# Row factor of the attention probabilities folded into their two float16 passes (units 16 to 47)

## The chip, the cores and the metric

The kernel runs on one core of one Trainium2 chip. The metric is device time in microseconds of one execution of the whole program. [...]

## The reference

Three stages follow each other: a windowed attention, a first feed-forward layer, and a second one with its own normalisation.

```python
# q, k, v: 4 x 8 x 576 x 64; heads 0 to 3: window of 32; heads 4 to 7: the same, dilated by 4
scores = where(mask, scale * q @ k.T, -1e9)
attn = exp(scores - max(scores)); attn = attn / (sum(attn) + 1e-9)
x = (attn @ v) as 2304 x 512
h = x @ w_in                    # 512 x 2048
x = (h - tanh(h)) @ w_out       # 2048 x 512
h = x @ w_in2                   # 512 x 1024
sm = softmax(h); solu = h * sm
out = (layer_norm(solu) * g_ln) @ w_out2
```

## The kernel before

The 2304 tokens are cut into six groups of 384. The attention of a group is eight units, so there are 48 units, and a unit is four blocks of 96 queries by 128 keys. Units 0 to 7 run at the start, alone. All later units run between the matmuls of the first feed-forward layer, by a plan of slots: the layer has 96 steps of two slots, the even slot with the 12 matmuls of `mm1` (L485), the odd one with the 12 of `mm2` (L512, five steps behind). A unit has four slots, and every sixteenth slot holds the products with v of four units (`pv_pe`, L407). Each engine works its instructions off in the order in which the slots issue them.

From unit 16 on, a unit u goes through these stations.

- `prep_unit` (L289 on ScalarE, L290 and L292 on VectorE) makes a high and a low float32r part of q and k (units 20 to 47), tile `qks`.
- `qk_half` (L328, twice per unit, `half0` and `half1`) multiplies them into PSUM, and VectorE adds the mask and takes the row's bound (L337, L340) into the tile `p`.
- `sm_exp` (L348, ScalarE) makes the four blocks of `p` into exponentials, with a row sum each.
- `sm_norm` (L353 and L355 on VectorE) makes the factor `rs` from the sums, one number for each row and block. Then L357 on GpSimd multiplies `p` by it in place, 96x512 in one instruction. For units 16 and up the factor has 2^-14 in it, which `pv_pe` takes out later.
- `p_hi` (L366, ScalarE) casts `p` to float16 into the first half of the tile `pab`, one instruction of 96x512. `p_lo` (L371, VectorE) subtracts that from `p` into the second half, again one of 96x512.
- A transposing DMA (L374, issued by SyncE's queue) brings `pab` into `ptt`, and `p_sum` (L379, VectorE) adds the two parts into `pt`, which TensorE uses in L407.

The plan places `p_hi` one slot and `p_lo` two slots behind `sm_norm`, and `p_sum` three slots behind `p_lo`. `p` and `pab` share a ring of three buffers. As the built program has it, `pab` of a unit takes the buffer that `pab` of the unit before had: `p_hi` of unit u+1 waits for the landing of unit u's transposing DMA.

Beside this, every step of the layer has four passes over 128x384: tanh (L493, ScalarE), a subtraction (L496, VectorE), a cast (L499, ScalarE) and a second subtraction (L502, VectorE), which feed `mm2` five steps later. PSUM has two banks for `mm1`, two that the units' scores and products with v share (released by L340 and by L417), and four for `mm2`.

Units 20 to 39 also carry a load and a maximum over a piece of a later weight (L188, L208). After the sixteen steps of each group the results of `mm2` are copied out (L518, L520) and their maxima taken (L245).

Of the kernel before, what the change touches and what calls it, by code (L numbers as in the profile page):

```python
# [13 lines left out]
AF = mybir.ActivationFunctionType  # L14
ALU = mybir.AluOpType
# [9 lines left out]
NQ, NK = 96, 128  # L25
# [15 lines left out]
def tile_kernel(ctx: ExitStack, tc: tile.TileContext, qk, vw, cst, w_in, w_out, w_in2, w_out2, g_ln, out):  # L41
    nc = tc.nc
# [124 lines left out]
    DT = 2 * NU  # L167
# [183 lines left out]
    def sm_norm(u):  # L351
        d = un[u]
        nc.vector.tensor_scalar(out=d["rs"], in0=d["sm"], scalar1=1e-9, scalar2=2.0 ** -14 if u >= DT else 1.0,  # L353
                                op0=ALU.add, op1=ALU.mult)
        nc.vector.reciprocal(out=d["rs"], in_=d["rs"])  # L355
        eng = nc.vector if u == NU - 1 else nc.gpsimd
        eng.tensor_tensor(out=d["p"], in0=d["p"],  # L357
                          in1=d["rs"].unsqueeze(2).to_broadcast([NQ, 4, NK]), op=ALU.mult)
# [4 lines left out]

    def p_hi(u):
        d = un[u]
        nc.scalar.copy(out=d["ab"][:, 0:4 * NK], in_=d["p"].rearrange("p b k -> p (b k)"))  # L366

    def p_lo(u):
        d = un[u]
        ab = d["ab"]  # L370
        nc.vector.tensor_tensor(out=ab[:, 4 * NK:], in0=d["p"].rearrange("p b k -> p (b k)"), in1=ab[:, 0:4 * NK],  # L371
                                op=ALU.subtract)
        d["tt"] = at_p.tile([NK, 2, 4, NQ], F16, tag="ptt", name=f"ptt{u}")
        nc.sync.dma_start_transpose(out=d["tt"].rearrange("p a b q -> p (a b) q"), in_=ab)  # L374

# [62 lines left out]
    for r in range(NU + 3):  # L438
        t = qk_f32(r, st_ps, "qk") if r < NU else None
        b1 = pv_pe(r - 4, st_ps, "pv") if r % 2 == 0 and 0 <= r - 4 < NU else None  # L440
        b2 = tr_pe(r - 2, st_ps, "tr") if 0 <= r - 2 < NU else None
        if t:
            t()
        if back:
            back("h")
        if t:
            sm_exp(r)
        if 0 <= r - 1 < NU:
            sm_norm(r - 1)
        if back:  # L450
            back("l")
        back = b1
        if b2:
            b2()
        if r in SW:
            w_step(dve=True)
        if r in (4, 5):
            load_v(r + 2)
        if r in (6, 8):
            load_unit(NU + r // 2 - 3)  # L460
# [76 lines left out]
    def plan():  # L537
# [3 lines left out]
        for u in range(u0, u1 + 2):  # L541
            p = 4 * u - 41 if u >= 2 * NU else (2, 6, 8, 12, 14, 16, 18, 20)[u - u0]
            q = p + 2 if u >= 2 * NU or u < u0 + 4 else p + 1
            if u < u1:
                at(p + 1, lambda u=u: preps.extend(prep_unit(u + 1)))
                for i in (1, 1, 2):
                    at(p + i, lambda: preps.pop(0)() if preps else None)
                if u < NFU:
                    piece(p, lambda u=u: qk_f32(u, a_ps, "at"))
                    at(p + 1, lambda u=u: sm_exp(u))  # L550
                    at(p + 2, lambda u=u: sm_norm(u))
                else:
                    piece(p, lambda u=u: qk_half(u, 0, a_ps, "at"))
                    at(p + 2, lambda u=u: sm_exp(u, (0, 1)))
                    piece(p + 1, lambda u=u: qk_half(u, 1, a_ps, "at"))
                    at(p + 3, lambda u=u: sm_exp(u, (2, 3)))
                    at(p + 4, lambda u=u: sm_norm(u))
                i = u - NFU
                if 0 <= i < 20:
                    at(p - 1, lambda u=u, i=i: sc_load(u + 2, i))  # L560
                    at(p + 1, lambda u=u, i=i: sc_max(u + 2, i))
                if i == 20:
                    at(p - 1, lambda u=u: new_qk(u + 2))
                    at(p - 1, lambda u=u: sc_rows(u + 2))
                    piece(p + 1, lambda: sc_pe(a_ps, "at"))
                at(p + 1, lambda u=u: load_unit(u + 2))
            if DT <= u < u1:
                for i, fn in ((3, p_new), (5, p_hi), (6, p_lo), (9, p_sum)):
                    at(p + i, lambda u=u, fn=fn: fn(u))
# [497 lines left out]
```

## Time and profile before

| | us |
|---|---|
| median of 3 runs (lowest, highest) | 682.93 (682.88, 683.92) |
| the profiled execution | 683.13 |
| its span | 681.3 |
| TensorE busy | 661.0 (97%) |
| VectorE busy | 532.6 (78%) |
| ScalarE busy | 386.3 (57%) |
| GpSimd busy | 174.5 (26%) |

The changed instructions lie between 110 and 410 us of the span. The busy time of an engine is the union of its instructions' times; consecutive instructions of one engine overlap a little, so distances from start to start are shorter than durations.

### The profile page before, as it was taken

To read this page: it belongs to the slowest core of one execution; us is meant where nothing else is said; L and a number is where in the kernel's file an instruction comes from. 1 tells how busy PE (TensorE), PEld (TensorE's weight loads), DVE (VectorE), ACT (ScalarE), POOL (GpSimd) and SP (SyncE) were. 2 spreads that over 40 slices of the span, in tenths; PEclk is the share of its full clock that TensorE was granted. 3 is DMA by queue.
4 is the path that set the end of the run, shared out by engine and by line. 5 is a ranking of instruction groups with operands and counts; after the bars stand their busy time and mean duration, and the time that the engine had idled before them with its cause. 6 is when DMAs were issued, how large, how long until landed. Compare 5 with 4: busy or idle time off the path is not lost. (4 is left out here: it accounts for less than half of the span.)

```text
span 681.3 us, 11184 instructions
## 1 busy us (share of the span) xinstructions
PE 661.0 (97%) x3882; PEld 547.9 (80%) x3882; DVE 532.6 (78%) x1315; ACT 386.3 (57%) x917; POOL 174.5 (26%) x174
## 2 busy tenths in 40 slices
PE   6998999999999999999999999999999999999997
PEld 5787899999999999999999999999954444444443
DVE  5988657679888997999888963499978877777751
ACT  5778757545555655555565532475636645555442
POOL 2302311110111110101111010266314656644411
PEclk9999989999999999999999999999999999999999
DMA  9977632254545555454434211453412555433233
GB/s 284 353 233 213 199 105 55 82 158 117 141 121 149 159 147 149 126 176 107 110 93 110 54 25 49 146 192 124 155 46 63 124 124 123 94 81 74 67 89 92
DMA packets 93608, 87.09 MB, mean 128 GB/s; under 512 B 62192, under 2 KB 78064, under 8 KB 93552
## 3 DMA queue, kind: packets, MB, share of 16 engines
q1 hardware_dynamic: 90384, 81.67, 43.5%
q10 hardware_dynamic: 3168, 4.72, 1.9%
q8 instruction: 30, 0.49, 0.3%
q14 instruction: 26, 0.21, 0.1%
HBM read 62.25 MB, written 9.44 MB: 105 GB/s over the span
## 5 line engine op out<-in xcount | busy, mean ns | idle before, releaser
L485 PE MATMUL h<-x,wi 128*128 128x384 f32 x1152 | 218.7, 339 | 0.8 <-DVE t L496 0.8
L512 PE MATMUL y<-gs,wo 128*128 128x384 f32 x1152 | 217.9, 339 | 0.0
L485 PEld LDWEIGHTS h<-x,wi 128*128 128x128 f32 x1152 | 201.1, 190 | 2.1 <-DVE t L496 1.0
L512 PEld LDWEIGHTS y<-gs,wo 128*128 128x128 f32 x1152 | 200.0, 189 | 1.9 <-issue 0.3
L357 POOL TENSOR_TENSOR p<-p,rs 96x512 f32<-96x512 f32 x47 | 58.6, 1247 | 341.8 <-DVE rs L355 328.8
L502 DVE TENSOR_TENSOR gs<-t,gs 128x384 fp32r<-128x384 f32 x96 | 81.1, 845 | 22.7 <-ACT gs L499 22.7
L931 PE MATMUL po<-w2o_o,zt 128*128 128x512 f16 x432 | 94.8, 379 | 0.0
L499 ACT CAST gs<-t 128x384 fp32r<-128x384 f32 x96 | 48.9, 510 | 76.5 <-DVE t L496 76.3
L348 ACT ACTIVATE p<-p,nm 96x128 f32<-96x128 f32 x192 | 74.8, 391 | 19.7 <-DVE nm L313 19.7
L931 PEld LDWEIGHTS <-zt 128*128 128x128 f16 x432 | 42.0, 98 | 51.0 <-DMA zt<-e 0.4
L496 DVE TENSOR_TENSOR t<-h,t 128x384 f32<-128x384 f32 x96 | 53.0, 552 | 33.5 <-ACT t L493 32.8
L779 PEld LDWEIGHTS <-yt 128*128 128x128 f16 x378 | 36.9, 98 | 47.0 <-issue 3.5
L493 ACT ACTIVATE t<-h 128x384 f32<-128x384 f32 x96 | 46.3, 483 | 36.5 <-PE h L485 33.1
L854 ACT ACTIVATE e<-hn,sml 128x1024 f32<-128x1024 f32 x18 | 20.7, 1150 | 56.3 <-DVE sml L794 43.5
L779 PE MATMUL sp<-w2i_t,yt 128*128 128x512 f16 x216 | 48.6, 379 | 2.2 <-DVE u L817 2.2
L904 DVE SCALAR_TENSOR_TENSOR e<-hn,sml,e 128x1024 f16<-128x1024 f32 x18 | 25.6, 1426 | 19.6 <-ACT e L903 19.6
L779 PE MATMUL sp<-w2i_b,yt 128*128 128x512 f16 x162 | 37.9, 379 | 0.0
L308 PE MATMUL qkp<-qkr 64*96 64x128 f32 x160 | 29.9, 343 | 8.0 <-DMA qkr<-in_qk_dram 6.0
L366 ACT CAST pab<-p 96x512 f16<-96x512 f32 x32 | 19.8, 619 | 31.4 <-POOL p L357 23.4
L348 ACT ACTIVATION_READ_ACCUMULATOR p<-p,nm 96x1 f32 x192 | 36.0, 187 | 0.0
L308 PEld LDWEIGHTS qkp<-qkr 64*96 64x96 f32 x160 | 24.5, 208 | 12.6 <-DMA qkr<-in_qk_dram 5.6
L313 DVE CUSTOM_DVE_ANT_0 p<-qkp,cst_sb 96x128 f32<-96x128 f32 x80 | 18.3, 281 | 14.9 <-PE qkp L308 8.2
(116 smaller groups left out, 844.3 us busy)
## 6 DMA issues: line engine op xcount, KB each, us to landing
qkr<-in_qk_dram SPq DMA_DIRECT2D x28, 448.0 KB, 3.4
raw_wi<-in_w_in_dram SPq DMA_DIRECT2D x16, 511.8 KB, 7.0
raw_wo<-in_w_out_dram SPq DMA_DIRECT2D x16, 511.8 KB, 7.6
v<-in_vw_dram SPq DMA_DIRECT2D x48, 128.0 KB, 3.6
y_dr<-ys ACTq DMA_DIRECT2D x6, 768.0 KB, 3.9
yr<-y_dr SPq DMA_DIRECT2D x9, 512.0 KB, 4.2
out_dram<-o SPq DMA_DIRECT2D x18, 256.0 KB, 2.7
qkr<-in_qk_dram SPq DMA_DIRECT2D x20, 224.0 KB, 5.2
```

The lines of the kernel that those rows point to most:

```text
L308: nc.tensor.matmul(ps[:, b], d["r"][:64, b * NQ:(b + 1) * NQ], d["r"][:64, QC + b * NK:QC + (b + 1) * NK], start=True, stop=True)
L348: nc.scalar.activation(out=d["p"][:, b], in_=d["p"][:, b], func=AF.Exp, scale=-1.0, bias=d["nm"][:, b:b + 1], accum_out=d["sm"][:, b:b + 1])
L357: eng.tensor_tensor(out=d["p"], in0=d["p"], in1=d["rs"].unsqueeze(2).to_broadcast([NQ, 4, NK]), op=ALU.mult)
L485: nc.tensor.matmul(ps, w[:, a, k * 128:(k + 1) * 128], xt[g, k][:, b], start=(n == 0), stop=(n == 3 * KD - 1))
L493: nc.scalar.activation(out=t, in_=ps, func=AF.Tanh)
L496: nc.vector.tensor_tensor(out=t, in0=ps, in1=t, op=ALU.subtract)
L499: nc.scalar.copy(out=gs[:, 0], in_=t)
L502: nc.vector.tensor_tensor(out=gs[:, 1], in0=t, in1=gs[:, 0].bitcast(F32), op=ALU.subtract)
L512: nc.tensor.matmul(yb[g][m], wo[c][:, a, m * 128:(m + 1) * 128], gs[:, b], start=(c == 0 and i == 0), stop=(c == NF - 1 and i == 2))
L779: nc.tensor.matmul(ps, y[:, a, blk, kk], w2i[w, kk][:, b], start=first and q == 0, stop=q == 5, skip_group_check=not first)
L904: nc.vector.scalar_tensor_tensor(out=ab[:, 1], in0=d["hn"], scalar=d["f"], in1=ab[:, 0], op0=ALU.mult, op1=ALU.subtract)
L931: nc.tensor.matmul(po, z[:, a, j], w2o[j][:, b], start=(q == 0), stop=(q == 3 * NF2 - 1))
```

## The change

For units 16 and up `sm_norm` stops after the reciprocal, so that GpSimd no longer multiplies `p`, and `p` keeps the plain exponentials. `p_hi` becomes four ScalarE instructions of 96x128, each with the factor of its block as the scale of the activation. `p_lo` becomes four VectorE instructions of 96x128 that multiply by the same factor and subtract the high part in one pass. Units 8 to 15 keep the multiplication on GpSimd. No other instruction is moved.

```diff
--- before.py
+++ after.py
@@ -353,6 +353,8 @@
         nc.vector.tensor_scalar(out=d["rs"], in0=d["sm"], scalar1=1e-9, scalar2=2.0 ** -14 if u >= DT else 1.0,
                                 op0=ALU.add, op1=ALU.mult)
         nc.vector.reciprocal(out=d["rs"], in_=d["rs"])
+        if u >= DT:
+            return
         eng = nc.vector if u == NU - 1 else nc.gpsimd
         eng.tensor_tensor(out=d["p"], in0=d["p"],
                           in1=d["rs"].unsqueeze(2).to_broadcast([NQ, 4, NK]), op=ALU.mult)
@@ -363,13 +365,17 @@
 
     def p_hi(u):
         d = un[u]
-        nc.scalar.copy(out=d["ab"][:, 0:4 * NK], in_=d["p"].rearrange("p b k -> p (b k)"))
+        for b in range(4):
+            nc.scalar.activation(out=d["ab"][:, b * NK:(b + 1) * NK], in_=d["p"][:, b], func=AF.Copy,
+                                 scale=d["rs"][:, b:b + 1])
 
     def p_lo(u):
         d = un[u]
         ab = d["ab"]
-        nc.vector.tensor_tensor(out=ab[:, 4 * NK:], in0=d["p"].rearrange("p b k -> p (b k)"), in1=ab[:, 0:4 * NK],
-                                op=ALU.subtract)
+        for b in range(4):
+            nc.vector.scalar_tensor_tensor(out=ab[:, (4 + b) * NK:(5 + b) * NK], in0=d["p"][:, b],
+                                           scalar=d["rs"][:, b:b + 1], in1=ab[:, b * NK:(b + 1) * NK], op0=ALU.mult,
+                                           op1=ALU.subtract)
         d["tt"] = at_p.tile([NK, 2, 4, NQ], F16, tag="ptt", name=f"ptt{u}")
         nc.sync.dma_start_transpose(out=d["tt"].rearrange("p a b q -> p (a b) q"), in_=ab)
 
```

The order on ScalarE around the high part of unit 30 was this. A name is followed by its unit and a running number; in brackets stand the counters that an instruction waits on. `DMAHW6` counts the landing of unit 29's transposing DMA here: the instruction that adds the transposed parts of unit 29 waits on it too.

```order
L366 CAST pab30_2866<-p30_2773 96x512 [waits DMAHW6_49,Pool_49]
L289 CAST qks32_2919<-qkr32_2758 128x896 [waits DMAHW4_49]
L493 ACTIVATE t42_2906<-h42_2893 128x384 [waits PE_49]
L348 ACTIVATE p31_2881,sm31_2883<-p31_2881,nm31_2882 96x128 [waits DVE_49] x2
L499 CAST gs42_2907<-t42_2906 128x384 [waits DVE_49]
L348 ACTIVATE p31_2881,sm31_2883<-p31_2881,nm31_2882 96x128 x2
```

With the change the same place reads as follows (lines from L374 on have moved by six).

```order
L369 ACTIVATE pab30_2936<-p30_2838,rs30_2841 96x128 [waits DMAHW6_49,DVE_49,Activation_49]
L369 ACTIVATE pab30_2936<-p30_2838,rs30_2841 96x128 [waits Activation_49] x3
L289 CAST qks32_2991<-qkr32_2823 128x896 [waits DMAHW4_49]
L499 ACTIVATE t42_2975<-h42_2962 128x384 [waits PE_49]
L348 ACTIVATE p31_2951,sm31_2953<-p31_2951,nm31_2952 96x128 [waits DVE_49] x2
L505 CAST gs42_2976<-t42_2975 128x384 [waits DVE_49]
```

One instruction has become four, the wait for GpSimd is gone, the wait for the DMA has stayed, and the cast of q and k for unit 32 (L289) still stands right behind. The other waits on ScalarE's own counter are for the exponentials of the same blocks, issued several instructions before.

On VectorE the place of unit 30's low part was this.

```order
L496 TENSOR_TENSOR t42_2906<-h42_2893,t42_2906 128x384 [waits Activation_49]
L371 TENSOR_TENSOR pab30_2866<-p30_2773,pab30_2866 96x512 [waits Pool_49]
L292 TENSOR_TENSOR qks32_2919<-qkr32_2758,qks32_2919 128x512
L502 TENSOR_TENSOR gs42_2907<-t42_2906,gs42_2907 128x384 [waits Activation_49]
L496 TENSOR_TENSOR t43_2962<-h43_2949,t43_2962 128x384 [waits Activation_49]
```

With the change it is this.

```order
L502 TENSOR_TENSOR t42_2975<-h42_2962,t42_2975 128x384 [waits Activation_49]
L376 SCALAR_TENSOR_TENSOR pab30_2936<-p30_2838,rs30_2841,pab30_2936 96x128 x4
L292 TENSOR_TENSOR qks32_2991<-qkr32_2823,qks32_2991 128x512
L508 TENSOR_TENSOR gs42_2976<-t42_2975,gs42_2976 128x384 [waits Activation_49]
L502 TENSOR_TENSOR t43_3037<-h43_3024,t43_3037 128x384 [waits Activation_49]
```

The four passes stand in the place of the one, ahead of L292, which completes the operands of unit 32's scores.

## Rows read from the trace of the kernel before

**Rows 1.** Busy time by stretch: stretch, length, then each engine's busy time, clock, DMA

```profile
110.00:410.00 300.00, 299.99 (x1947) 294.47 (x1946) 253.06 (x703) 167.33 (x467) 35.33 (x33) 1.00 0.44 117
```

**Rows 2.** One line's instructions, GpSimd, L357: duration in ns, least/median/most

```profile
L357 POOL TENSOR_TENSOR p<-p,rs x47: 1037/1039/2378, 10.7 to 401.2; 96x512 f32<-96x512 f32 x47
```

**Rows 3.** Timeline, 240 to 252 us: start, length, engine, line, operation, tiles, [idle before]

```profile
240.86 0.68 DVE L371 TENSOR_TENSOR pab<-p,pab 96x512 f16<-96x512 f32 x1
...
241.46 0.68 DVE L292 TENSOR_TENSOR qks<-qkr,qks 128x512 fp32r<-128x512 f32 x1
241.60 1.21 SPq L374 DMA_TRANSPOSE ptt<-pab  x1
...
242.13 0.55 DVE L502 TENSOR_TENSOR gs<-t,gs 128x384 fp32r<-128x384 f32 x1
...
243.68 1.04 POOL L357 TENSOR_TENSOR p<-p,rs 96x512 f32<-96x512 f32 x1 [7.54 <-DVE rs L355]
...
243.81 1.32 DVE L502 TENSOR_TENSOR gs<-t,gs 128x384 fp32r<-128x384 f32 x1 [0.30 <-ACT gs L499]
244.75 0.62 ACT L366 CAST pab<-p 96x512 f16<-96x512 f32 x1 [0.97 <-POOL p L357]
...
245.28 0.94 ACT L289 CAST qks<-qkr 128x896 fp32r<-128x896 f32 x1
...
246.51 0.56 DVE L290 TENSOR_TENSOR qks<-qkr,qks 64x384 fp32r<-64x384 f32 x1
...
248.98 0.68 DVE L371 TENSOR_TENSOR pab<-p,pab 96x512 f16<-96x512 f32 x1
```

**Rows 4.** Timeline, TensorE, first halves of the scores of units 31 to 34

```profile
243.47 0.40 PE L328 MATMUL qkp<-qks 128*96 128x256 f32 x2
...
252.29 0.40 PE L328 MATMUL qkp<-qks 128*96 128x256 f32 x2
...
261.10 0.40 PE L328 MATMUL qkp<-qks 128*96 128x256 f32 x2
...
271.59 0.40 PE L328 MATMUL qkp<-qks 128*96 128x256 f32 x2
```

**Rows 5.** One line, L374: the transposing DMAs from issue to landing

```profile
DMA to landing us min/median/max: 2.8/2.9/4.8
```

**Rows 6.** Timeline, 148 to 173 us: two high parts that waited for a landing

```profile
148.73 1.21 SPq L374 DMA_TRANSPOSE ptt<-pab  x1
...
153.28 0.62 ACT L366 CAST pab<-p 96x512 f16<-96x512 f32 x1 [2.07 <-DMA ptt<-pab]
...
168.33 1.22 SPq L374 DMA_TRANSPOSE ptt<-pab  x1
...
172.99 0.62 ACT L366 CAST pab<-p 96x512 f16<-96x512 f32 x1 [2.49 <-DMA ptt<-pab]
```

**Rows 7.** Single lines: durations in ns, least/median/most, of like instructions elsewhere

```profile
L627 DVE SCALAR_TENSOR_TENSOR w2o_o<-f,gl,w2o_o x8: 739/744/1229, 460.3 to 494.2; 128x512 f16<-128x512 f32 x8
...
L904 DVE SCALAR_TENSOR_TENSOR e<-hn,sml,e x18: 1271/1285/1744, 513.3 to 665.6; 128x1024 f16<-128x1024 f32 x18
...
L348 ACT ACTIVATE p<-p,nm x192: 384/388/405, 6.8 to 397.8; 96x128 f32<-96x128 f32 x192
```

**Rows 8.** Timeline, 148 to 179 us: VectorE's last work before TensorE's scores

```profile
148.59 0.68 DVE L292 TENSOR_TENSOR qks<-qkr,qks 128x512 fp32r<-128x512 f32 x1
...
149.81 0.40 PE L328 MATMUL qkp<-qks 128*96 128x256 f32 x2
...
159.89 1.02 DVE L417 SCALAR_TENSOR_TENSOR x<-pv,x 128x384 fp32r<-128x384 f32 x2
160.50 0.48 PE L328 MATMUL qkp<-qks 128*96 128x256 f32 x2
...
177.56 0.68 DVE L292 TENSOR_TENSOR qks<-qkr,qks 128x512 fp32r<-128x512 f32 x1
...
178.38 0.45 PE L328 MATMUL qkp<-qks 128*96 128x256 f32 x2
```

## The prediction

> **What bounds the kernel now.** I read the busy time by stretch first. Between 110 and 410 us, where all the changed instructions lie, TensorE works for 299.99 of 300.00 us at its full clock, while VectorE has 253.06, ScalarE 167.33 and GpSimd 35.33 [rows 1]. So in this stage the time is TensorE's instruction stream, and nothing that another engine saves can make it shorter. Another engine can only make it longer, by handing something over too late. The question of this change is therefore: which hand-over to TensorE is tightest, and how do the new passes move it?
>
> TensorE's own rhythm comes from the starts of the units' first scores: 243.47, 252.29, 261.10, 271.59 [rows 4]. A plain unit takes 8.82 us of TensorE, and one with the products with v 10.49. One unit in four is of the second kind, so the mean is (3 x 8.82 + 10.49) / 4 = 9.24 us.
>
> Next I followed one unit through the timeline [rows 3], from the low part of unit 29 (L371, start 240.86) to that of unit 30 (248.98). The point to see there is a loop that goes round once per unit, through three engines. The low part ends at 241.54, and the transposing DMA is issued at 241.60. Its landing frees the buffer into which the next unit's high part (L366) is written, 2.8 to 4.8 us later, median 2.9 [rows 5]. The high part starts at 244.75, L289 behind it at 245.28 (0.53 from start to start), and it runs for 0.94. VectorE needs its result in L290 (246.51), and 2.47 us after L290's start the next low part starts. In sum 0.68 + 0.06 + 2.9 + 0.04 + 0.53 + 0.94 + 0.03 + 2.47 = 7.65 us, with 0.04 and 0.03 as estimates for the hand-overs to ScalarE and VectorE, of the size of the 0.06 between 241.54 and 241.60. That is 1.2 us below TensorE's 8.82, so the loop bounds nothing today, and in the row itself L366 was released by GpSimd, not by the DMA. But twice early in the stage it waited for the landing, 2.07 and 2.49 us [rows 6].
>
> The last thing to see is how little room the hand-over itself has. Behind each low part L292 completes the operands of the scores of two units later. It ends at 149.27 and TensorE's scores start at 149.81; it ends at 178.24 and they start at 178.38 [rows 8]. In the second case the scores start 0.14 after L292's end, which I take as the least distance. In the first there is thus 0.4 us to spare.
>
> **The change part by part.**
>
> *GpSimd's multiplication goes, 32 of the 47 [rows 2].* Its least duration is 1.04 us, but GpSimd is not what TensorE waits for: on that engine it is worth nothing. Two things end with it. L366 no longer waits for it (0.97 us), and L502 no longer runs beside it: L502 took 1.32 us beside GpSimd's instruction, 0.55 without it [rows 3]. That gives VectorE 0.77 us per unit. The cover that makes this worth nothing is TensorE's full stretch [rows 1].
>
> *The low part becomes four passes.* The like instruction, with a factor from memory, float32 in and float16 out, takes 744 ns at 512 elements and 1285 at 1024 [rows 7], that is 1.057 ns per element, so 744 - 384 x 1.057 = 338 ns at 128. On VectorE an instruction starts 0.08 us before its forerunner ends (240.86 + 0.68 against 241.46 [rows 3]). Four passes take 4 x 0.338 - 3 x 0.08 = 1.11 us to the last result against 0.68: **+0.44** in the loop, the same ahead of L292, and the same on VectorE. VectorE as a whole gets shorter (-0.77 + 0.44). Bounds for the four: 0.68 us (no cost per pass, as the one of 512 elements) and 1.35 us (4 x 0.338, no overlap). I take 1.11, since the overlap is seen in the very place.
>
> *The high part becomes four activations.* L348 is the nearest row: 96x128 with an operand per row, 388 ns [rows 7]. ScalarE overlaps by 0.09 us (244.75 + 0.62 against 245.28). L289 then starts 4 x (0.388 - 0.09) = 1.19 us after the first of them instead of 0.53: **+0.66** in the loop. Bounds: 0.53 us (no cost per piece) and 1.55 us (no overlap); I take 1.19 for the same reason. ScalarE itself has the time: 167 of 300 us busy.
>
> *The sum.* The loop becomes 7.65 + 0.44 + 0.66 = **8.75 us** at the median landing, 8.65 at the least, and 10.65 at the longest. TensorE's plain unit is 8.82. What was a margin of 1.2 us is none: every landing above 3.0 us makes the loop late, and it catches up only in the unit with the products. Around it, the end of each group adds copies and maxima (L518, L245) to VectorE's part of the loop, about 2 us in eight units. Units 40 to 47 have no L208 and a loop of some 8.2.
>
> What this costs TensorE I worked through by hand, unit by unit, with the landings of this trace. Unit 19's DMA was issued at 148.73 and its successor's high part waited until 153.28 [rows 6]; now the issue is 0.44 later, the activations take 0.66 more, and unit 20's low part and all behind it on VectorE come 1.1 to 1.5 later. Its L417, which frees a PSUM bank for the scores at 160.50, started at 159.89 [rows 8], and these scores already stand right behind the end of its first instruction. They move by 1.5 us. Unit 21's long landing (168.33 to 172.99 [rows 6]) delays unit 22 by a further 1.1: L292 ends not at 178.24 but near 180.7, TensorE is by then late by 1.5 itself, and loses about 1.0 more. After that the lateness stays and makes room; the next losses are small (0.1 at unit 25, 0.7 and 0.1 at the group ends of units 29 and 37), and a third long landing, at unit 38, costs 1.1. Together 4.5 us. If all landings took 2.9, the first two losses and the last would vanish, and about 1 us would be left at the tight places. Which landings are long is chance (the longest is 1.9 above the median, and I see no cause), so I take 3.0 us, between the two. Behind 410 us TensorE has no idle time that could give it back.
>
> The profiled execution took 683.13 us, 0.2 above the median of the runs. 683.13 + 3.0 = 686.1, against the median 685.9.
>
> [...] The rows at hand give a 128-element pass 338 ns (VectorE) and 388 ns (ScalarE). [...]
>
> **The rivals.**
> *Not slower: the loop stays below TensorE's unit.* VectorE is relieved by 0.77 us per unit and reaches each wait earlier; if the pieces cost half of what I added (0.22 and 0.33) and the landings are mostly at 2.8, the loop is 7.55 + 0.55 = 8.10 us, and TensorE's scores are never late; with the full pieces and no long landing near a tight place only the small losses are left. It decides at 8.82. For it: the row of 241.60 landed in time, and the median landing is 2.9. Against it: rows 6. The time would be 682.9 to 684.3. Even then it is hardly faster: the stretch can give back only what TensorE waits in it, the 0.01 us of rows 1 and the two late starts of rows 8, some 0.3 us together: 682.6.
> *Much slower: the pieces do not overlap.* With 1.35 and 1.55 us the loop is 9.35 at the median landing, above even the mean unit of 9.24. Then TensorE follows the loop. With the group ends' 2 us in eight units, units 20 to 39 would lose 20 x (9.35 + 0.25 - 9.24) = 7.2 us, and the early losses (2.5) come on top: 683.13 + 9.7 = 692.8. Against it: both overlaps are seen wherever two instructions stand side by side.
>
> **How the numbers follow.** A measurement of this kernel can tell about 0.2% (1.4 us) from no change. The forecast, a loop as long as TensorE's unit with losses of 1.4 to 6.5 us, gets 0.60; much slower 0.10; not slower 0.30, of which 0.04 for a time below by more than 0.2% and 0.26 within. That makes 0.04 faster, 0.26 same, 0.70 slower. The range takes in most of the first rival and the forecast's upper end: 683.0 to 690.0.
>
> **What would show it.** Right: four passes with starts 0.26 us apart and four activations 0.30 apart; L502 at 0.55 us everywhere in units 16 to 47; the high part's release changed from GpSimd to the landing in most of units 20 to 39; VectorE's L290 waiting for L289; idle time of TensorE before L328, in the stretch 140 to 340 us most of all; the distance of unit starts above 8.82 in some plain units. Wrong: TensorE at 300 of 300 us as before, or starts of the low parts 8.82 apart or less with landings of 3 us; a loss that lies behind 410 us; or TensorE waiting for another tile than the scores' operands or the bank that L417 frees.

## The result, and the profile after

| us | before | after |
|---|---|---|
| median (lowest to highest, runs) | 683.42 (682.88 to 685.08, 4) | 690.73 (689.43 to 693.07, 4) |
| the profiled execution | 683.13 | 689.43 |
| its span | 681.3 | 687.3 |

The change makes the kernel slower: the ratio is 1.0096, with a 95% interval of 1.0072 to 1.0119. The forecast was 685.9, slower with a chance of 0.70. The side is right; the size was too small, and 690.73 lies 0.7 us above the end of the range.

**Where the 6.0 us of span arose.** I compared the start of TensorE's first matmul of each of the layer's 96 steps in the two traces. The kernel after is 1.62 us late by step 7 (67.77 us in before), and stays at 1.62 until step 21. From step 22 on, in the stage between 140 and 420 us, it falls back a further 4.00. The tail adds 0.4. The first 1.62 lies ahead of the stage: the first changed instruction of the program, the high part of unit 16, already starts 1.5 us late itself.

The first high part in the timeline of the kernel before:

```profile
110.76 0.61 ACT L366 CAST pab<-p 96x512 f16<-96x512 f32 x1
```

In that of the kernel after:

```profile
112.30 1.28 ACT L369 ACTIVATE pab<-p,rs 96x128 f16<-96x128 f32 x4
```

No changed instruction has run by then. What differs is TensorE's granted clock. The row of the kernel before (columns as in [rows 1]), then that of the kernel after:

```profile
61.00:64.40 3.40, 3.40 (x21) 3.26 (x19) 3.15 (x7) 3.16 (x7) 1.91 (x1) 1.00 0.51 199
```

```profile
61.00:64.40 3.40, 3.40 (x13) 3.40 (x12) 3.09 (x7) 3.15 (x7) 1.91 (x1) 0.50 0.24 98
```

In the kernel after the granted clock is 0.50 of full here, and TensorE, busy throughout in both, has 13 matmuls in this stretch where the kernel before has 21. Just before, from 55 to 60 us, it was busy 2.76 and 2.78 of 5 us, the same in both. The kernel before has one such stretch ahead of the stage (86.0 to 89.4 us, 0.50), the kernel after a second one like it (88.3 to 91.7, 0.50) besides this one. It does not hang on the change alone: the profile of the changed kernel with four more loads (below) has full clock from 61 to 64 us, and the kernel before with an unused tile has the half clock there.

In the profiles of the experiments the early lateness lies between -1.1 and 5.2 us (at step 20), and the time of the kernel before scatters as well: 22 later runs of it lay between 682.99 and 688.93. Much of that scatter goes with the clock: of all 63 later runs of it, the 19 with a mean granted clock of 0.997 have a median of 683.39 us, the 33 with 0.994 or 0.995 one of 684.83. So 4.0 us is what this profile charges to the change in the stage, and the repetitions below give 3.6 and 4.4.

**The stage by stretch**, in the changed kernel (columns as in [rows 1]):

```profile
140.00:180.00 40.00, 38.79 (x249) 37.69 (x249) 31.12 (x100) 22.22 (x67) 0.00 (x0) 1.00 0.46 130
180.00:220.00 40.00, 39.30 (x255) 38.54 (x254) 34.16 (x110) 25.33 (x77) 0.00 (x0) 1.00 0.53 146
220.00:260.00 40.00, 40.00 (x260) 39.41 (x259) 33.80 (x112) 25.94 (x79) 0.00 (x0) 1.00 0.51 147
...
300.00:340.00 40.00, 39.51 (x255) 38.48 (x254) 34.50 (x119) 24.40 (x79) 0.00 (x0) 1.00 0.48 128
...
380.00:420.00 40.00, 39.41 (x255) 38.69 (x254) 27.57 (x91) 20.60 (x62) 0.99 (x2) 1.00 0.17 34
```

TensorE, the first number behind the comma, was at 299.99 of 300 us [rows 1]. Now it idles 1.21, 0.70, 0.49 and 0.59 us in four of these stretches, at full clock. The loss is made of six short stops, 2.99 us in sum. That is less than 4.0 because the records of neighbouring matmuls overlap: twelve of them fill 2.25 us but start 2.09 apart from the next twelve, so a stop uses up 0.16 us of overlap before idle time shows. Six times 0.16 is nearly all of the missing 1.0.

**The new pieces.** From the groups by line of the kernel after:

```profile
L508 DVE TENSOR_TENSOR gs<-t,gs 128x384 fp32r<-128x384 f32 x96 | 58.9, 614 | 22.7 <-ACT gs L505 22.7
...
L369 ACT ACTIVATE pab<-p,rs 96x128 f16<-96x128 f32 x128 | 41.0, 391 | 19.1 <-DMA ptt<-pab 17.6 <-DVE p L337 0.9 <-DVE gs L508 0.6
...
L376 DVE SCALAR_TENSOR_TENSOR pab<-p,rs,pab 96x128 f16<-96x128 f32 x128 | 36.1, 342 | 0.0
```

The activations take 391 ns (388 forecast from [rows 7]), the passes of the low part 342 (338 forecast). L508, which is L502 of before, takes 0.55 us beside no GpSimd instruction, as [rows 3] had it.

**The loop**, in the timeline after, unit 30 to 31, beside [rows 3]:

```profile
253.34 1.13 DVE L376 SCALAR_TENSOR_TENSOR pab<-p,rs,pab 96x128 f16<-96x128 f32 x4
...
254.39 0.68 DVE L292 TENSOR_TENSOR qks<-qkr,qks 128x512 fp32r<-128x512 f32 x1
254.53 1.21 SPq L380 DMA_TRANSPOSE ptt<-pab  x1
...
257.47 1.28 ACT L369 ACTIVATE pab<-p,rs 96x128 f16<-96x128 f32 x4 [0.92 <-DVE p L337]
...
258.66 0.92 ACT L289 CAST qks<-qkr 128x896 fp32r<-128x896 f32 x1
...
259.62 0.56 DVE L290 TENSOR_TENSOR qks<-qkr,qks 64x384 fp32r<-64x384 f32 x1 [1.13 <-ACT qks L289]
...
262.08 1.12 DVE L376 SCALAR_TENSOR_TENSOR pab<-p,rs,pab 96x128 f16<-96x128 f32 x4
```

From low part to low part it is 8.74 us (262.08 - 253.34), in the next unit 8.70. The DMA of 254.53 landed at 257.37, and the next high part started 0.10 later. Its bracket names VectorE's L337, but that ended at 257.47 itself, too late to release anything; the landing, 0.10 before, is the releaser, at the same distance (0.08 to 0.11) as in 24 of the 31 units. L290 waits for L289. ScalarE, VectorE and the DMA stand in one chain.

**The waits**, VectorE and then ScalarE, 140 to 420 us (in all, times, longest). In the kernel before:

```profile
DVE qks L290 <- ACT qks L289: 2.8, 3, 1.0
```

```profile
ACT pab L366 <- POOL p L357: 23.4, 24, 1.0
```

In the kernel after:

```profile
DVE qks L290 <- ACT qks L289: 20.5, 22, 1.7
```

```profile
ACT pab L369 <- DMA ptt<-pab: 16.5, 18, 2.5
```

The high part's release has gone from GpSimd to the landing, as forecast, and VectorE now waits 20.5 us for the cast of q and k, where it waited 2.8.

**Three stops of TensorE.** The timeline after, 149 to 183 us, to be held beside [rows 6, 8]:

```profile
155.36 1.28 ACT L369 ACTIVATE pab<-p,rs 96x128 f16<-96x128 f32 x4 [2.09 <-DMA ptt<-pab]
...
157.51 0.56 DVE L290 TENSOR_TENSOR qks<-qkr,qks 64x384 fp32r<-64x384 f32 x1 [1.67 <-ACT qks L289]
...
158.37 0.88 PE L413 MATMUL pv<-pt,v 128*64 128x96 f32 x16
...
159.75 0.28 DVE L340 CUSTOM_DVE_ANT_0 p<-qkp,p 96x128 f32<-96x128 f32 x1
...
160.14 0.88 PE L413 MATMUL pv<-pt,v 128*64 128x96 f32 x16 [0.90 <-PE pv L413]
...
163.01 1.02 DVE L423 SCALAR_TENSOR_TENSOR x<-pv,x 128x384 fp32r<-128x384 f32 x2
163.62 0.47 PE L328 MATMUL qkp<-qks 128*96 128x256 f32 x2 [0.31 <-DVE x L423]
...
181.35 0.68 DVE L292 TENSOR_TENSOR qks<-qkr,qks 128x512 fp32r<-128x512 f32 x1
182.18 0.45 PE L328 MATMUL qkp<-qks 128*96 128x256 f32 x2 [0.70 <-ACT t L499]
```

Behind unit 19's long landing the scores that followed 159.89 in before now follow L423 at 163.62, 0.31 us late. 0.90 us more goes just before: the second half of the products with v (L413) stops, as I read it, at a PSUM bank. The profile puts that wait down to TensorE itself, but L413's first half was over by 159.25; the products share their two banks with the scores, and L340 reads scores out until 160.03, 0.11 before the start (at the like stop of 309.82 us it is 0.11 as well). So this bank, too, came late from VectorE. At 182.18 the wait is put down to ScalarE's L499; L292 ended at 182.03, 0.15 before, and 0.14 was the least distance in [rows 8].

### The profile page after: what moved, and what is told of

The parts are those of the page before. It is cut to its first block, busy times and chain, and to the rows that moved or that the text cites. A ratio compares the mean times of both kernels' runs of the same rounds, so it can differ in the third digit from the quotient of the medians.

```text
span 687.3 us, 11312 instructions
## 1 busy us (share of the span) xinstructions
PE 662.9 (96%) x3882; PEld 548.8 (80%) x3882; DVE 523.7 (76%) x1411; ACT 405.3 (59%) x1013; POOL 139.0 (20%) x142
## 5 line engine op out<-in xcount | busy, mean ns | idle before, releaser
L508 DVE TENSOR_TENSOR gs<-t,gs 128x384 fp32r<-128x384 f32 x96 | 58.9, 614 | 22.7 <-ACT gs L505 22.7
L502 DVE TENSOR_TENSOR t<-h,t 128x384 f32<-128x384 f32 x96 | 52.9, 551 | 30.5 <-ACT t L499 30.5
L499 ACT ACTIVATE t<-h 128x384 f32<-128x384 f32 x96 | 46.1, 481 | 36.0 <-PE h L491 32.7
L100 POOL MEMSET top<- 128x512 int32 x4 | 2.0, 526 | 289.7 <-PE qkp L328 289.7
L369 ACT ACTIVATE pab<-p,rs 96x128 f16<-96x128 f32 x128 | 41.0, 391 | 19.1 <-DMA ptt<-pab 17.6
L359 POOL TENSOR_TENSOR p<-p,rs 96x512 f32<-96x512 f32 x15 | 23.2, 1544 | 76.4 <-DVE rs L355 63.3
L376 DVE SCALAR_TENSOR_TENSOR pab<-p,rs,pab 96x128 f16<-96x128 f32 x128 | 36.1, 342 | 0.0
```

The costliest lines, as they stand in the source:

```text
L369: nc.scalar.activation(out=d["ab"][:, b * NK:(b + 1) * NK], in_=d["p"][:, b], func=AF.Copy, scale=d["rs"][:, b:b + 1])
L376: nc.vector.scalar_tensor_tensor(out=ab[:, (4 + b) * NK:(5 + b) * NK], in0=d["p"][:, b], scalar=d["rs"][:, b:b + 1], in1=ab[:, b * NK:(b + ...
L499: nc.scalar.activation(out=t, in_=ps, func=AF.Tanh)
L502: nc.vector.tensor_tensor(out=t, in0=ps, in1=t, op=ALU.subtract)
L508: nc.vector.tensor_tensor(out=gs[:, 1], in0=t, in1=gs[:, 0].bitcast(F32), op=ALU.subtract)
```

## The experiments

All are edits of one of the two kernels, and each comparison is with the kernel before, run on the same chip.

**The cast of q and k ahead of the high part.** In the changed kernel only the order on ScalarE differs: `p_hi` of a unit is issued behind the preparations of that slot, so that L289 no longer stands behind the four activations.

```diff
+                if DT < u:
+                    at(p + 1, lambda u=u: p_hi(u - 1))
...
+            if u == u1:
+                at(p + 1, lambda u=u: p_hi(u - 1))
...
-                for i, fn in ((3, p_new), (5, p_hi), (6, p_lo), (9, p_sum)):
+                for i, fn in ((3, p_new), (6, p_lo), (9, p_sum)):
```

> The changed kernel with one edit: on ScalarE the cast of q and k (L289) stands ahead of the four activations of the high part instead of behind them. Theory (the loop low part, landing, high part, L289, L290, low part has become as long as TensorE's unit): the cast no longer waits for the landing, the loop that is left goes through tanh and L496 and is 1.19 + 2.8 + 0.10 + 1.19 + 0.5 + 0.5, about 6.3 us against TensorE's 8.82, so the waits of TensorE before L328 between 140 and 410 us go from 4.0 us to under 0.7 us, L290's wait for L289 (20.5 us) goes to under 5 us, and the time returns to within 2.5 us of the kernel before. Rival A (the four passes ahead of L292 on VectorE are late by themselves, 0.44 us each unit, the loop does not matter): these passes stay, TensorE still loses 3 us or more in this stretch. Rival B (most of the 7 us lies outside the stretch, in the loading phase before 70 us, because the program has more instructions): the time stays 4 us or more above the kernel before.

Measured: 685.14 (12 runs) against 684.9 (22 runs), ratio 0.9996 [0.9980, 1.0012]. The stage loses nothing: step 20 starts 0.09 us after that of the kernel before, step 80 0.11 before it. By stretch:

```profile
140.00:180.00 40.00, 40.00 (x259) 39.11 (x258) 34.48 (x110) 25.01 (x76) 0.00 (x0) 1.00 0.51 146
180.00:220.00 40.00, 40.00 (x260) 39.52 (x259) 33.35 (x107) 25.20 (x75) 0.00 (x0) 1.00 0.47 137
```

All pieces of the change are in this kernel, with their durations (the high part 1.28 us as in the changed kernel), and units 17, 19 and 21 have landings above 4 us here too. What is missing is the path from the landing through the four activations to L289. So it is not the eight pieces nor the long landings that cost time, but the loop in which they stand: this is the forecast's mechanism, shown, and the rivals of this experiment fall.

**Two DMAs for one.** The high part is transposed by a DMA of its own as soon as it is written, the low part by a second.

```diff
+        d["tt"] = at_p.tile([NK, 2, 4, NQ], F16, tag="ptt", name=f"ptt{u}")
+        nc.sync.dma_start_transpose(out=d["tt"][:, 0], in_=d["ab"][:, 0:4 * NK])
...
-        nc.sync.dma_start_transpose(out=d["tt"].rearrange("p a b q -> p (a b) q"), in_=ab)
+        nc.sync.dma_start_transpose(out=d["tt"][:, 1], in_=ab[:, 4 * NK:])
```

> The changed kernel with the transposing DMA cut in two: that of the high part is issued right behind the high part, that of the low part behind the low part; buffer, passes and order on ScalarE and VectorE stay. Theory: the next high part now waits for a landing whose DMA was issued some 4 us earlier, so the wait of L369 for the landing (16.5 us between 140 and 420 us) goes to under 3 us, the loop opens, TensorE's waits before L328 in this stretch fall from 4.0 to under 0.7 us, and the time is within 2.5 us of the kernel before, unless the queue of SyncE, which now issues 32 DMAs of 1.2 us more, holds up the loads. Rival A (four passes ahead of L292): no change against the changed kernel. Rival B (loading phase): 4 us or more above before.

Measured: 686.93 (11 runs), ratio 1.0041 [1.0026, 1.0056], and 2.2 us lost in the stage. The loop was not opened, against my expectation: the next high part waits for both landings (it starts 0.10 to 0.16 us behind the second in 17 of 31 units, and 3.5 us or more behind the first), since the buffer is guarded as a whole. But the second DMA is half as large, and its median landing is 2.3 us, from the line of the low part's DMA:

```profile
DMA to landing us min/median/max: 2.3/2.3/4.2
```

In the timeline the loop is shorter by that half microsecond, from high part to high part 191.27 - 183.07 = 8.20:

```profile
183.07 1.30 ACT L369 ACTIVATE pab<-p,rs 96x128 f16<-96x128 f32 x4 [0.41 <-DMA ptt<-pab]
...
188.85 1.18 SPq L381 DMA_TRANSPOSE ptt<-pab  x1
191.27 1.28 ACT L369 ACTIVATE pab<-p,rs 96x128 f16<-96x128 f32 x4 [0.36 <-DMA ptt<-pab]
```

The miss turned into a useful point between the other two: with a loop of 8.7 us the stage loses 4.0, with 8.2 it loses 2.2, and without the loop nothing.

**One part in four, the other in one.** The kernel before with four activations by a factor of one, and with four low passes alone. The factor came from a new tile of 16 bytes per row.

```diff
+    one = const.tile([128, 4], F32, name="one")
+    nc.gpsimd.memset(one, 1.0)
...
+        for b in range(4):
+            nc.scalar.activation(out=d["ab"][:, b * NK:(b + 1) * NK], in_=d["p"][:, b], func=AF.Copy,
+                                 scale=one[:NQ, b:b + 1])
```

> The kernel before, GpSimd still multiplying, with the high part alone in four activations of 96x128 with a factor of one from memory. Theory: the loop is 7.65 + 0.66 = 8.3 us, still below 8.82, so TensorE waits at most 0.7 us more in the stretch than in the kernel before and the time is within 1.5 us of it. Rival A: the low part is whole, so the same: no loss. A third reading (every added instruction on ScalarE costs TensorE something, with no threshold): half of the loss, 2 us or more.

> The kernel before, GpSimd still multiplying, with the low part alone in four passes of 96x128 with a factor of one from memory. Theory: the loop is 7.65 + 0.44 = 8.1 us, below 8.82; VectorE, still disturbed by GpSimd in L502, needs about 8.1 + 0.44 = 8.6 us per unit; TensorE loses 0.4 us at the tight hand-overs (units 21, 24, 29, 37, 45), together 0.5 to 2 us. Rival A (the four passes ahead of L292 are what costs): 3 us or more in the stretch, as in the changed kernel or worse.

Measured: 693.25, 1.0123 [1.0102, 1.0143], and 691.98, 1.0109 [1.0088, 1.0130]. Both are far above what my theory had, and only the two readings without an upper end (2 us or more, 3 us or more) would allow them. Two things were mixed in. One is the tile: the distance from one of TensorE's matmuls of `mm1` to the next is 175.7 ns in both, against 173.9 before. The other is what GpSimd's multiplication does to a unit's turn, which I had overlooked (below). So these two say nothing on the pieces by themselves. I ran them again without the tile, with the row sums `sm` as the factor, and then both together.

> The kernel before, GpSimd still multiplying, with the high part alone in four activations, their factor read from the row sums that are there already (no new tile, so that no other tile changes its place as in the two earlier runs; the probabilities come out multiplied by their row sum, in the high part alone). Theory now with a second loop: L290, low part, L502, L496, L353, L355, GpSimd, high part, L289, L290, which takes 8.12 to 8.32 us in the kernel before; with 0.66 more it is 8.8 to 9.0, above TensorE's 8.82, and TensorE's matmuls of the first layer begin to come late by 1.5 to 4.5 us in the stretch 110 to 410 us. Without that second loop (my first reading) under 0.7 us.

> The kernel before, GpSimd still multiplying, with the low part alone in four passes, factor from the row sums (the low part comes out otherwise than in the reference). Second loop 8.12 to 8.32 + 0.44 = 8.56 to 8.76, just below 8.82, and 0.44 less room ahead of L292: 0.5 to 3 us lost in the stretch, less than with the high part in four. Rival A (the four passes ahead of L292 cost most): more than with the high part in four.

> High and low part both in four, and GpSimd's multiplication kept (factor from the row sums). The second loop is 8.2 + 1.1 = 9.3 to 9.4 us, above even the mean unit of 9.24: TensorE loses more than in the changed kernel, 6 to 12 us in the stretch. That would show that taking GpSimd out saved some 4 us of what the eight pieces cost. If the pieces alone decide and GpSimd's part is worth nothing, the loss is that of the changed kernel, 4 to 5 us.

```diff
+            nc.scalar.activation(out=d["ab"][:, b * NK:(b + 1) * NK], in_=d["p"][:, b], func=AF.Copy,
+                                 scale=d["sm"][:, b:b + 1])
```

| kernel before, and ... | median | ratio | lost in the stage |
|---|---|---|---|
| four activations | 690.51 (4 runs) | 1.0097 [1.0070, 1.0124] | 5.7 |
| four low passes | 688.22 (7 runs) | 1.0072 [1.0045, 1.0099] | 4.0 |
| both, GpSimd still multiplying | 701.24 (4 runs) | 1.0251 [1.0210, 1.0291] | 15.9 |

(The last column is how far the start of the steps falls back between step 20 and step 80, as above.) All three lost more than I had expected (1.5 to 4.5, 0.5 to 3, and 6 to 12). With GpSimd kept, half of the pieces cost as much as the whole change without it. Of the 15.9 us some 1.6 are the clock's: from 405 to 410 us it is 0.74 in that profile, after TensorE had stood still for 1.91 us, and twelve matmuls take 3.89 us instead of 2.25:

```profile
407.08 3.89 PE L516 MATMUL y<-gs,wo 128*128 128x384 f32 x12
```

The other kernels have the full clock in the stage. The timeline of the kernel with both shows what stands in a unit's turn:

```profile
250.91 1.13 DVE L374 SCALAR_TENSOR_TENSOR pab<-p,sm,pab 96x128 f16<-96x128 f32 x4
251.96 0.68 DVE L292 TENSOR_TENSOR qks<-qkr,qks 128x512 fp32r<-128x512 f32 x1
252.10 1.21 SPq L378 DMA_TRANSPOSE ptt<-pab  x1
254.10 1.04 POOL L357 TENSOR_TENSOR p<-p,rs 96x512 f32<-96x512 f32 x1 [8.29 <-DVE rs L355]
255.17 1.28 ACT L367 ACTIVATE pab<-p,sm 96x128 f16<-96x128 f32 x4 [0.97 <-POOL p L357]
256.36 0.93 ACT L289 CAST qks<-qkr 128x896 fp32r<-128x896 f32 x1
257.32 0.56 DVE L290 TENSOR_TENSOR qks<-qkr,qks 64x384 fp32r<-64x384 f32 x1 [0.43 <-ACT qks L289]
```

There is a second loop. Behind the low part VectorE goes through L292, two passes of the layer and L353 and L355; then comes GpSimd (1.04), the high part, L289, and L290, from which VectorE comes to the next low part. The landing is not in it. Beside it stands VectorE's own stream, in which L506 takes 1.33 us beside GpSimd (as L502 in [rows 3]). In the kernel before the two are nearly even. L290 starts at 246.51 [rows 3] and then, 8.32 us later, without idle time ahead of it:

```profile
254.83 0.56 DVE L290 TENSOR_TENSOR qks<-qkr,qks 64x384 fp32r<-64x384 f32 x1
```

So VectorE's own stream sets that turn. How often L290 waits for L289 between 140 and 420 us tells which of the two has become the longer: with four activations 26 times (15.9 us in all), the loop; with four low passes 4 times (3.9; in the kernel before 3 times, 2.8), so there it is VectorE's own stream; with both 26 times (15.7). The low parts of the last kernel start at 250.91 and 259.79, 8.88 us apart, with a maximum of the layer (L249) in that turn. Its other plain turns take 8.80, so TensorE's 8.82 leaves nothing to make up what a long landing or the end of a group puts late. How the loss divides between the loop and VectorE's own stream no run here separates.

The change takes GpSimd out of both. Without GpSimd the eight pieces cost 3.6 to 4.4 us in the stage, with it some 14 (15.9 less the clock's 1.6). So the removal, worth nothing alone (next run), gave back some 10 us of what the pieces would have cost.

**GpSimd's multiplication alone taken away.** The kernel before without L357 for units 16 and up, high and low part in one instruction each; the factor is left out of these units.

```diff
+        if u >= DT:
+            return
```

> The kernel before without GpSimd's multiplication for units 16 to 47 and with the high and the low part in one instruction each (the probabilities of these units stay unnormalised). Both loops are short (7.65 and about 7.0 us), L502 takes 0.55 us everywhere: TensorE waits for nothing in the stretch, 0 to 0.3 us are gained there, and the time is that of the kernel before within 0.2%: the relief of VectorE and GpSimd is worth nothing by itself.

Measured: 684.73 (10 runs), ratio 1.0000 [0.9979, 1.0021], and nothing lost or won in the stage (0.71 us late at step 20, 0.47 at step 80). VectorE works 217.38 us of the 280 between 140 and 420, where the kernel before has 237.40. Twenty microseconds of VectorE are worth nothing here, as the prediction had it.

**The tile alone.** The kernel before with the 16 bytes of `one`, which nothing reads.

> The kernel before with one more constant tile of 16 bytes per partition and its memset, used by nothing; every later tile of that side of the memory starts 16 bytes further. The two runs with a tile of ones showed TensorE's starts drifting by 0.04 us per step all along, and 175.7 ns from matmul to matmul instead of 173.9. If the place of the tiles does that, this run shows the same pace (175 to 176 ns in steps 20 to 60) and is 3 to 5 us slower than the kernel before; if it came from the added pieces, the pace is 173.9 and the time that of before.

Measured: 688.17 (10 runs) against 684.88 (17 runs), ratio 1.0047 [1.0029, 1.0064]. TensorE is busy throughout the stage, at full clock, and its steps drift apart by 0.04 us each in the mean. Rows of twelve matmuls in its timeline:

```profile
252.94 2.28 PE L514 MATMUL y<-gs,wo 128*128 128x384 f32 x12
...
255.29 2.26 PE L487 MATMUL h<-x,wi 128*128 128x384 f32 x12
```

The same rows in the kernel without GpSimd's multiplication and without the tile:

```profile
253.12 2.25 PE L487 MATMUL h<-x,wi 128*128 128x384 f32 x12
...
255.44 2.25 PE L514 MATMUL y<-gs,wo 128*128 128x384 f32 x12
```

So an unused tile cost 3.3 us. The changed kernel has no new tile and its pace is 173.9 ns; this is no part of its loss.

**The changed kernel again**, and with four more loads ahead of the stage.

> The changed kernel once more, unchanged, beside the kernel before. If the long landings (4.4 to 4.6 us) stand at fixed places of the program, units 17, 19 and 21 have them again and the loss in the stretch is again 4 us; if they fall by chance, they stand elsewhere and the loss is between 1 and 6 us. The ratio to the kernel before should lie between 1.006 and 1.011.

Measured: 689.41 (6 runs) against 684.88 (17 runs), ratio 1.0069 [1.0042, 1.0095]; 3.6 us lost in the stage, and landings of 4.5, 4.5 and 4.4 us at units 17, 19 and 21 once more.

```diff
-        nc.sync.dma_start(out=v.rearrange("p b h d -> p (b h d)"), in_=vw[u])
+        for _ in range(2 if 12 <= u < 16 else 1):
+            nc.sync.dma_start(out=v.rearrange("p b h d -> p (b h d)"), in_=vw[u])
```

> The changed kernel, with the v tiles of units 12 to 15 loaded twice: four more transfers of 128 KB on SyncE's queue before 115 us, all before unit 16's transposing DMA and none in the stage where the loss lies. In the kernel before and in each changed kernel with one transposing DMA per unit, units 19 and 21 had landings of 4.3 to 4.7 us. Theory 1, the long landings belong to a count of what SyncE's queue has carried: they move off units 19 and 21 to other units; then the 1.4 and 0.7 us that TensorE lost at steps 24 and 28 go, unless the new long ones fall on units just as tight: the loss between 140 and 410 us is 1.5 to 3 us instead of 3.6 to 4.0, and the time 687 to 689. Theory 2, they belong to the place in the program (what else moves there): units 19 and 21 keep landings above 4.3 us, the loss stays at 3.6 to 4.0, and the time is that of the changed kernel, 689 to 691. Unit 17, long in two profiles of the changed kernel with no other transfer near it, speaks for theory 1; unit 22, with the same transfers around it as unit 21 and a landing of 2.8 us, too.

Measured: 689.78 (5 runs) against 684.47 (8 runs), ratio 1.0071 [1.0047, 1.0095]. Theory 2 holds: the landings of units 17, 19 and 21 stay at 4.4 us, and the stage loses 4.4. So which landings are long early in the stage does not move with four more transfers in the queue. What makes them long no experiment shows, but the traces have a strong hint that I had overlooked: the expectation says that unit 17's landing has no other transfer near it, and it has one. From 129 to 134 us of the kernel after the queues and the DMA issues are these:

```profile
q1 hardware_dynamic: 800, 0.20, 20.9%
q8 instruction: 1, 0.02, 1.2%
...
ptt<-pab SPq DMA_TRANSPOSE x1, 4.5
```

One packet of the queue that the profile calls `instruction` moves while the transposing DMA is under way (from 2.4 us after its issue, for 1.0). In the twelve profiles of kernels with one transposing DMA per unit, 59 of the 384 landings took more than 4.0 us, and all 59 have such a packet in them; the longest of the 277 landings without one took 3.8. A packet alone does not make a landing long, as the 107 that have one go from 2.8 to 4.8, and no run moved these packets.

These three profiles of changed kernels give one more reading. Unit 44's landing differs between them: 3.5, 3.7 and 4.4 us. TensorE's stop that follows, before the spread of the scale of `mm2`'s results (L227, for which VectorE's L249 comes late behind the low part and L292), grows with it. In the changed kernel:

```profile
395.67 0.68 PE L227 MATMUL ysp<-cst_sb,ym 128*128 128x128 f32 x4 [0.59 <-DVE ym L249]
```

In its repetition:

```profile
395.62 0.68 PE L227 MATMUL ysp<-cst_sb,ym 128*128 128x128 f32 x4 [0.84 <-DVE ym L249]
```

With the four loads:

```profile
395.94 0.68 PE L227 MATMUL ysp<-cst_sb,ym 128*128 128x128 f32 x4 [1.45 <-DVE ym L249]
```

0.9 us more landing, 0.86 us more stop: at this tight place, where no slack was left, a late landing went into the time nearly one for one.

## Why the prediction was right, and where it was too small

- **TensorE bounds, and the question is the tightest hand-over.** Right: taking 20 us of VectorE and 32 instructions of GpSimd away moved nothing, and moving one ScalarE instruction ahead of another took the whole loss away.
- **The prices of the pieces.** Right: 342 and 391 ns for 338 and 388; passes 0.26 us apart (1.13 for four), activations 0.30 apart (1.28 for four).
- **The loop of 8.75 us.** Right: 8.74 and 8.70, with landings of 2.8 where 2.9 was reckoned; the step from the landing to the high part took 0.10 where the estimate was 0.04, and the two cancel.
- **The hand-worked loss of 4.5 us.** Near: 4.0, 3.6 and 4.4 in three profiles, in part by luck. Step 24, behind unit 19's landing, cost 1.34 to 1.40 (1.5 worked out), and step 28, behind unit 21's, 0.69 to 0.71 (1.0). But the group ends of units 29 and 37 (0.7 and 0.1 in the working) cost nothing, and unit 38's landing (1.1) was short in all three. In their stead two places cost that the working did not have: step 56, near 310 us, with 0.96, 0.31 and 0.42 (the first behind a landing of 3.8 us at unit 35), and step 74, near 396 us, with 0.71, 0.97 and 1.57 (behind unit 44's landing, long in the trace of before already, 4.5 us, and not in the working).
- **"Which landings are long is chance ... so I take 3.0."** This step failed. The trace of before showed long landings at units 19 and 21 [rows 6], and I took half of their price off because I saw no cause. In all twelve profiles of kernels with one transposing DMA per unit, these two took 4.3 us or more. They belong to the program, and a cost that stands in the trace should have been taken as it stands: 4.5, which gives 687.6 for the profiled execution, where 689.4 was measured. In the three profiles of the changed kernel only the later ones (32 to 44) vary, and the third landing that I had priced, at unit 38, was not long again in them.
- **What TensorE waits for.** Partly right: I had named the scores' operands and the bank that L417 frees, and held any other tile for a sign of being wrong. Two stops were others: the bank that L340 frees, for the products with v, and L249's maxima, 0.6 to 1.5 us. Both hang on the same late VectorE.
- **The loop through GpSimd.** Not seen as a loop, though its release of L366 stood in [rows 3]. For this change it made no error, since the change removes it; for the half changes it made my expectations too low.
- **The rest of the difference.** 690.73 - 683.42 = 7.3 us in the first comparison, 4.5 and 5.3 in the two later ones. Above the 3.6 to 4.4 of the stage and 0.4 of the tail, the first comparison has some 2.5 us. The prediction has no term for the clock ahead of the stage, and 1.6 us of the profiled execution arose there, at a granted clock of 0.50, before any changed instruction. At a mean granted clock of 0.994 or 0.995 the changed kernel's seven runs have a median of 689.43 us, the 33 of the kernel before 684.83: 4.6 apart. So, as an estimate, the change is worth 4.6 us, and the first comparison had some 2.7 of chance in it. Whether the change makes a stretch of lower clock more likely no run here says.

## What to carry to other kernels

Where one engine is full, look for the loops that hand work round through the others, count each per turn, landing of DMAs included, and compare with the full engine's turn: here an edit on "free" engines cost nothing while the loop was well below that length, and as the distance went each late landing cost at the next tight hand-over. It did not need to be all gone: beside TensorE's 8.82 us a loop through the landing of 7.65 cost nothing, one of 8.2 cost 2.2 us, one of 8.7 cost 4.0. The cure here was not a faster instruction but another place for one that did not belong to the loop and stood in its queue. And a delay that a trace shows at a place should be priced in full there until a second trace shows that it moves: of the three long landings that the prediction priced, two stayed in all twelve profiles, and the third came in five.

## What the runs showed of the hardware that I had not expected

- An unused tile of 16 bytes per row, allocated ahead of others, slowed TensorE's matmuls from 173.9 to 175.8 ns each in the stage, at full clock, and the kernel by 3.3 us. Why is open; TensorE waits for nothing there.
- The transposing DMAs of units 19 and 21 land 4.3 to 4.7 us after issue in all twelve profiles with one DMA per unit, while the median is 2.8, and unit 22, with the same kinds of data transfers around it as unit 21, has 2.8 in the kernel after. Every landing above 4.0 us in these profiles has an `instruction` packet in it; unit 22's has none. That the packet is the cause is not shown.
- A stretch of TensorE at a granted clock of 0.50 between 61.0 and 64.4 us (13 matmuls where the kernel before has 21 at 1.00) made the changed kernel 1.6 us late in its profile, before any changed instruction had run.
